# A decode kernel for grouped-query attention beside a Mish layer: no critical section at the start, and the first load of wq shared by two queues

## The chip, the cores and the metric

The kernel runs on one core of a Trainium2 chip. The core has five engines, each with its own instruction stream: TensorE (PE, matrix products; PEld are its weight loads), VectorE (DVE), ScalarE (ACT), GpSimd (POOL) and SyncE (SP). Sixteen DMA engines move data between HBM and the on-chip memory SBUF, which has 128 partitions; here SyncE and ScalarE issue DMAs, each on a queue of its own (q1 and q10 in the profile). PSUM holds the products of TensorE. The metric is the device time of one execution in microseconds (us), the median of the timed runs.

## The reference

For 8 sequences with one new token each: a layer norm of x (8 x 512), then the sum of x, an attention over a cache of 8192 positions, and a dense layer with the Mish activation. All is float32.

```python
def _A_ref(x, k_cache, v_cache, wq, wo):          # B=8, Sq=1, D=512
    Hq, Dh = 32, 128                               # 8 KV heads, 4 query heads each
    q = (x @ wq).reshape(B, Sq, Hq, Dh).transpose(0, 2, 1, 3)
    k = jnp.repeat(k_cache, rep, axis=1)           # k_cache, v_cache: (8, 8, 8192, 128)
    v = jnp.repeat(v_cache, rep, axis=1)
    scores = jnp.einsum("bhqd,bhkd->bhqk", q, k) * (Dh ** -0.5)
    p = softmax(scores, axis=-1)
    o = jnp.einsum("bhqk,bhkd->bhqd", p, v)
    return o.transpose(0, 2, 1, 3).reshape(B, Sq, Hq * Dh) @ wo

def _B_ref(x, w1, b1, w2):                         # F=1792
    h = jnp.einsum("bsd,df->bsf", x, w1) + b1
    return jnp.einsum("bsf,fd->bsd", h * jnp.tanh(softplus(h)), w2)

xn = layernorm(x)
return x + _A_ref(xn, k_cache, v_cache, wq, wo) + _B_ref(xn, w1, b1, w2)
```

The two caches are 268 MB each, and each of their elements is used once.

## The kernel before

**Tiling.** The work goes in 16 packs. A pack takes a pair of KV heads (`PAIRS` = 4) and two of the eight sequences (`PB` = 2, `NP` = 4). For each pack and each of its two sequences `b` one load brings K (128 partitions x 64 KB, 8.4 MB) and one brings V (as much). So the stream of the kernel is 64 such loads, and between them the weights: wq and wo in four pieces of 2 MB each, w1 and w2 with 3.7 MB each.

**Places in SBUF.** There are three big buffers. `kva` (place "a") holds 64 KB in each partition: w1 first, then the second K of pack 0, K(0,1), then the V's. `kvb` ("b") holds 80 KB, a quarter more than a load, so that the next K may be issued when three quarters of the one before have been read. `kvw` ("w") holds a piece of wq or wo.

**Order of the loads.** `plan` puts a load into a list, in the order in which the loads are to run; `pump` issues from the head of the list as long as the place of the head is free; `release`, called behind the last product that reads a place, frees it and calls `pump`. All loads in the list are issued by SyncE, which executes its DMAs in that order and waits ahead of each for a semaphore of the engine that read the place last. The order at the start is wq(0), w1, K(0,0), K(0,1), K(1,0), V(0,0), K(1,1), V(0,1), and so on. x (16 KB) and b1 (7 KB) are issued by ScalarE, on its own queue, at the head of the program.

**V(0,0).** One load is treated apart: `load_early`, called in the middle of the products of K(0,1), takes the head of the list, which is the second half of V(0,0), and issues it into the half of `kva` that these products have read by then. The first half of V(0,0) follows behind the last product of K(0,1).

**How the program is written out.** Every instruction is first recorded as an `Op` by `Program.add`, which works out from the regions read and written who has to wait for whom; `issue` (line 383 is the call in it that makes the instruction, so that nearly every row of the profile has that line) writes it out with its wait. `emit_first` writes out those instructions of the part ahead of the loop that stand before the first wait of their engine, among them the first DMAs and some memsets, inside a critical section of the framework (lines 1135 and 1138):

```python
    prog.prepare()
    with tc.tile_critical(no_gpsimd_drain=True):
        prog.emit_first()
    tc.close()
```

The framework puts a hand-over between engines at both ends of such a section, and a barrier at `tc.close()`. `emit` writes out the rest: what is ahead of the loop over packs 1 to 15, the loop for TensorE, VectorE and ScalarE, and the end.

**The start, step by step.** `setup` clears some tiles, computes the layer norm of x on VectorE (the first instruction that reads x is a reduction of `sc`, 8 x 512, into `st`), transposes it on TensorE and makes the selection matrices out of an identity. GpSimd copies the normalised x in another order, TensorE transposes that as well (`setup_w1`). `queries` multiplies with wq(0) into `H`; VectorE scales, transposes and copies it to `qc`, and `expand` makes `qT`, the weights for the scores. `mish` starts with the product of the selection `gsel` with b1 and goes on with w1; when its last product is done, `kva` is free for K(0,1). Then come `scores` of K(0,0), which are copied by ScalarE, `rows`, and `scores` of K(0,1). TensorE does all its products in that order.

Of the kernel before, what the change touches and what calls it, by code (L numbers as in the profile page):

```python
# [12 lines left out]
P = 128  # L13
# [9 lines left out]
G = 4  # L23
# [4 lines left out]
CC = D // P  # L28
# [11 lines left out]
HE = P // 2  # L40
V8 = PB * REP

KR = DH * 2 * NB // P
# [66 lines left out]
class Program:  # L110
# [260 lines left out]
            top[c] = max(n * self.unit[c], top.get(c, 0))  # L371
        return list(top.items())

    def issue(self, o, pack):
        engine = getattr(self.nc, o.engine)
        *first, last = self.values(o) or [None]
        for c, n in first:
            engine.wait_ge(self.sems[c], n)
        if o.method in ("settle", "relay"):
            got = engine.wait_ge(self.sems[last[0]], last[1])  # L380
        else:
            args, kw = (o.make(pack), {}) if o.make else (o.args, o.kw)
            got = getattr(engine, o.method)(*args, **kw)  # L383
            if last:
                got.wait_op(self.sems[last[0]], last[1], "sem-ge")
        if c := self.channel(o):
            got.then_inc(self.sems[c], o.unit)

    def emit_first(self):

        waiting = set()
        for o in self.ops:
            if o.waits:
                waiting.add(o.engine)
            if o.engine not in waiting and o.place[1] == "before":
                self.issue(o, o.pack)
                self.done.add(o)

    def emit(self):
        nc, issue, lower = self.nc, self.issue, self.lower  # L400
        for o in self.ops:
            if o not in self.done and (o.place[1] == "before" or o.engine not in LOOPED):
                issue(o, o.pack)
        for engine, parts in self.bodies():
            e = getattr(nc, engine)
            mine = [c for c in self.low if c[1] == engine]
            for c, n in (*self.low.items(), *self.early.items()):
                if c[1] == engine:
                    lower(engine, c, n)
            with e.Fori(FIRST, END) as pack:  # L410
                for ops, at in parts:
                    if name := ops[0].part:
                        with e.If_eq(e.to_reg(SOMETIMES[name](pack)), 0):
                            for o in ops:
                                issue(o, pack)
                            for c, k in self.drops.get((engine, "loop", at), {}).items():
                                lower(engine, c, max(k))
                        e.end_ifs()
                    else:
                        for o in ops:  # L420
                            issue(o, pack)
                for c in mine:
                    lower(engine, c, self.round[c])
            for o in self.ops:
                if o.place[1] == "after" and o.engine == engine:
                    issue(o, o.pack)
# [15 lines left out]
def kernel(  # L442
# [13 lines left out]
    prog = Program(nc)  # L456
    pe, dve, act, pool, sp = (getattr(prog, e) for e in ("tensor", "vector", "scalar", "gpsimd", "sync"))
# [12 lines left out]
    queue = []  # L470
    taken, landed, held = {}, {}, {}

    def rows_of(blocks):

        return blocks.rearrange("j p f -> (j p f)").rearrange("(p f) -> p f", p=P)

    def pump():

        while queue and taken.get(queue[0][1]) in (None, queue[0][0]):
            what, at, load = queue.pop(0)  # L480
            taken[at] = what
            landed[what] = load()

    def load_early():

        what, _, load = queue.pop(0)
        landed[what] = load()

    def release(what, relay=None):

        at = next(at for at, w in taken.items() if w == what)
        del taken[at]
        if relay:
            held[at] = [relay]
        pump()

    def plan(what, at, blocks, stream, part=(0, 1), lo=0):

        rows = rows_of(blocks)
        n = rows.shape[1]  # L500
        t = place[at][:, lo : lo + n]

        cols = slice(round(part[0] * n), round(part[1] * n))

        def load():
            sp.dma_start(t[:, cols], rows[:, cols], stream=stream, to="tensor", after=held.pop(at, ()))
            return t

        queue.append((what, at, load))

    sc = tile_of([P, 512], "sc")
    x_sb = sc[:B, :]
    act.dma_start(x_sb, x, stream="x", to="vector")

    acc = tile_of([P, D], "acc")
    b1_sb = acc[:G, :FG]
    act.dma_start(b1_sb, b1.rearrange("(g f) -> g f", g=G), stream="b1", to="tensor")

    def blocks_of(src, p, b):
        i, k = divmod(p, NP)  # L520
        lo = ((k * PB + b) * HKV + 2 * i) * NB
        return src[lo : lo + KN]
# [3 lines left out]
    def plan_k(p, b):  # L526
        blocks = blocks_of(kT, p, b)
        if (p, b) == (0, 1):
            plan(("k", p, b), "a", blocks, "k1")
        else:  # L530
            up[0] = KX * BW - up[0]
            plan(("k", p, b), "b", blocks, "k" if p else "k0", lo=up[0])

    def plan_v(p, b, at, stream="v", part=(0, 1)):
        plan(("v", p, b), at, blocks_of(v, p, b), stream, part)

    def plan_wq(i):
        plan(("wq", i), "w", wq[i * CC : (i + 1) * CC], "w")

    def plan_wo(i, stream="w", part=(0, 1)):  # L540
        plan(("wo", i), "w", wo[i * 4 : i * 4 + 4], stream, part)

    plan_wq(0)
    plan("w1", "a", w1, "w1")
    between = {}
    for i in range(1, PAIRS):
# [2 lines left out]
    for p in range(PACKS):  # L549
        for b in range(PB):  # L550
            plan_k(p, b)
            if (p, b) in between:
                what, i = between[p, b]
                (plan_wq if what == "wq" else plan_wo)(i)
            if p == 1 and b == 0:
                plan_v(0, 0, "a", "v1", (1 / 2, 1))
                plan_v(0, 0, "a", part=(0, 1 / 2))
            elif p > 0:
                plan_v(p - 1, b, "a")
    plan_v(PACKS - 1, 0, "b", "v0")  # L560
    plan_v(PACKS - 1, 1, "a", "va", (0, 3 / 4))
# [142 lines left out]
    def setup_w1(xs):  # L704
        for r in range(W1R):
            last = pe.transpose(
                M[:, 64 + r * B : 64 + (r + 1) * B], xs[:, r * P : (r + 1) * P], ident[:B, :B]
            )
        read = prog.relay("vector", "gpsimd", last)
        for t in range(2):  # L710
            dve.tensor_scalar(
                xw[:, :, t, :],
                M[:, 64 : 64 + W1R * B].rearrange("p (r b) -> p r b", r=W1R),
                half[:, t : t + 1],
                None,
                op0=ALU.mult,
            )

        pool.memset(pt, 0.0, after=[read], to="vector")
# [46 lines left out]
    def scores(b, k, order, first=False):  # L766

        t = qT[:, b].rearrange("p r u h -> p r (u h)")
        for r in order:
            if first and r == order[KR // 2]:  # L770
                load_early()
            for c in range(2):
                last = pe.matmul(
                    C[b][HE * c : HE * (c + 1), :],
                    t[:, r],
                    k[:, r * BW + c * 512 : r * BW + (c + 1) * 512],
                    start=(r == order[0]),
                    stop=(r == order[-1]),
                )
        read = prog.relay("scalar", "sync", last) if first else None  # L780
        act.copy(sc, C[b])
        return read
# [262 lines left out]

    prog.enter(0)
    pump()
    xs = setup()
    setup_w1(xs)
    read = queries(landed["wq", 0])  # L1050
# [5 lines left out]
    for p in range(PACKS):  # L1056
        prog.enter(p)
        for b in range(PB):
            k = landed.pop(("k", p, b))
            n = PB * p + b - (p > 0)  # L1060
            order = range(KR) if n % 2 == 0 else range(KR - 1, -1, -1)
            read = scores(b, k, order, first=(p, b) == (0, 1))
            release(("k", p, b), read)
            if p > 0 and b == 0:
# [21 lines left out]
            if (p, b) in between:  # L1086
                w = landed.pop(between[p, b])
# [16 lines left out]
    p = PACKS - 1  # L1104
# [27 lines left out]
    dve.tensor_copy(res, H[:, :P])  # L1132
    sp.dma_start(out, res, stream="out", to="sync")
    prog.prepare()
    with tc.tile_critical(no_gpsimd_drain=True):
        prog.emit_first()
    tc.close()
    tc.compile()
    prog.emit()
# [39 lines left out]
```

## Time and profile before

| | |
|---|---|
| median of 3 runs | 1304.92 us |
| lowest, highest run | 1304.13, 1305.15 us |
| profiled execution: time | 1304.17 us |
| profiled execution: span from first to last instruction | 1302.8 us |
| mean granted TensorE clock | 0.836 |
| TensorE / VectorE / ScalarE / GpSimd busy | 67% / 30% / 9% / 0% of the span |
| read from HBM | 561.01 MB, 431 GB/s over the span |
| chain that ended last | DMA 66%, PE 32%, DVE 1% |

The times of the profile are in us from the start of the span. "SPq" and "ACTq" are the sequencers of SyncE and ScalarE, which issue the DMAs; the duration in such a row is that of the issue, and the issue rows of the DMA view give the time from issue to landing. In a row of the timeline the start comes first, then the duration, the engine, the line and what is written from what; the bracket at the end tells how long the engine stood idle and who released it. "x16" is a count of instructions that were merged into one row. DMA packets are counted at their start, so a short stretch can show more than the engines can move.

### The profile page before, as it was taken

Reading aid. Unit: us, or ns where it says so; the run is one execution under the profiler, and the core shown is the slowest. Engines: PE = TensorE matmul, PEld = TensorE weight load, DVE = VectorE, ACT = ScalarE, POOL = GpSimd, SP = SyncE. Lnnn points to the kernel's source line nnn. Section 1 sums busy time; section 2 is a strip of 40 time slices with the busy share of each in tenths; the row PEclk is TensorE's granted clock in tenths of the full one; section 3 lists DMA queues with packets and bytes.
Section 4 is the critical chain, followed back from the end, with each engine's and each line's share of the span. In section 5 each row is a group of like instructions: output and inputs, shape, how many; then the busy total and the mean of one; then the engine's idle time right before and its main releaser. Section 6 shows DMA issues by size and latency. Waiting matters only on the chain.

```text
span 1302.8 us, 11368 instructions
## 1 busy us (share of the span) xinstructions
PE 874.2 (67%) x4814; PEld 279.6 (21%) x4814; DVE 389.9 (30%) x597; ACT 122.1 (9%) x294; POOL 4.8 (0%) x10
## 2 busy tenths in 40 slices
PE   4786657766667665686656686666876656766568
PEld 1221112212112221122211222111221221212113
DVE  6250504305051230521405133052320515115061
ACT  1020202001020100200102020020200102001020
POOL 1000000000000000000000000000000000000000
PEclk9887788887799877897887888778877779878889
DMA  9999999999999999999999999999999999999998
GB/s 402 447 423 436 429 439 431 431 437 431 439 429 441 425 443 425 434 433 437 431 433 437 420 450 427 443 425 443 423 441 429 437 431 433 435 431 439 429 432 363
DMA packets 11554, 561.22 MB, mean 431 GB/s; under 512 B 1292, under 2 KB 1424, under 8 KB 1560
## 3 DMA queue, kind: packets, MB, share of 16 engines
q1 hardware_dynamic: 11520, 561.06, 99.7%
q8 instruction: 7, 0.11, 0.0%
q10 hardware_dynamic: 24, 0.02, 0.0%
q14 instruction: 3, 0.02, 0.0%
HBM read 561.01 MB, written 0.07 MB: 431 GB/s over the span
## 4 chain that ended last, share of the span: by engine, by line
DMA 66%; PE 32%; DVE 1%; issue 0%; SPq 0%; ACT 0%; DVEq 0%
DMA kvb<-in_kT 65%; PE c L383 30%; DMA kvb<-in_w 2%; PE o L383 1%; DVE raw L383 0%; DVE pt L383 0%; SPq L383 0%; DVE os L383 0%; DVE nm L383 0%; PE s L383 0%; PE m L383 0%; PE h L383 0%; ACT sc L383 0%; DVE acc L383 0%; DVE nr L383 0%
## 5 line engine op out<-in xcount | busy, mean ns | idle before, releaser
L383 PE MATMUL c<-kvb,qT 128*64 128x512 f32 x1984 | 499.3, 667 | 330.9 <-DMA kvb<-in_kT 330.9
L383 PEld LDWEIGHTS c<-kvb,qT 128*64 128x64 f32 x1984 | 161.1, 154 | 669.1 <-issue 470.7
L383 PE MATMUL o<-kva,pt 128*32 128x512 f32 x1984 | 244.7, 650 | 24.7 <-DMA kva<-in_v 24.1
L383 DVE TENSOR_REDUCE nm<-s 128x1 f32<-128x1024 f32 x16 | 19.6, 1225 | 431.5 <-PE s L383 431.5
L383 DVE STREAM_TRANSPOSE raw<-wide 128x2048 f32<-128x2048 f32 x36 | 125.4, 3484 | 19.5 <-ACT wide L383 17.7
L383 ACT COPY sc<-c 128x512 f32<-128x512 f32 x32 | 18.7, 585 | 981.6 <-PE c L383 981.6
L383 PEld LDWEIGHTS o<-kva,pt 128*32 128x32 f32 x1984 | 65.8, 118 | 194.6 <-issue 151.9
L383 ACT ACTIVATE wide<-s,nms 128x512 f32<-128x512 f32 x128 | 88.0, 687 | 130.5 <-DVE nms L383 66.9
L383 DVE TENSOR_TENSOR oT<-m,rt 128x16 f32 (+1 forms) x17 | 3.0, 175 | 228.2 <-PE m L383 228.2
L383 DVE TENSOR_SCALAR os<-o,isel 128x128 f32<-128x128 f32 x32 | 11.2, 350 | 155.9 <-PE o L383 155.9
L383 DVE TENSOR_TENSOR pt<-raw 64x256 f32<-64x256 f32 x128 | 53.5, 418 | 1.9
L383 DVE TENSOR_TENSOR qT<-qc,bsel 128x1024 f32<-128x1024 f32 x34 | 40.2, 1222 | 17.5 <-PE s L383 17.4
L383 PE MATMUL s<-sc,csel 64*128 64x512 f32 x128 | 37.1, 657 | 8.5 <-ACT sc L383 7.1
L383 DVE TENSOR_TENSOR raw<-raw 128x1024 f32<-128x1024 f32 x32 | 39.2, 1225 | 2.9 <-DVE raw L383 0.2
L383 DVE SCALAR_TENSOR_TENSOR os<-o,isel,os 128x128 f32<-128x128 f32 x96 | 33.6, 351 | 3.4
L383 ACT ACTIVATION_READ_ACCUMULATOR wide<-s,nms 128x1 f32 x128 | 24.7, 193 | 0.0
L383 PE MATMUL m<-hsel,os 128*128 128x8 f32 x66 | 12.7, 265 | 10.6 <-DVE lsel L383 10.6
L383 PE MATMUL m<-ident,nm 128*1 128x128 f32 x16 | 4.4, 273 | 21.6 <-DVE nm L383 21.6
L383 DVE TENSOR_SCALAR wide<-h 128x512 f32<-128x512 f32 x16 | 11.1, 691 | 18.8 <-PE h L383 18.4
L383 PE MATMUL h<-kvw,xnT 128*64 128x512 f32 x64 | 16.5, 663 | 0.0
L383 PEld LDWEIGHTS m<-hsel,os 128*128 128x128 f32 x66 | 10.1, 193 | 25.3 <-issue 12.2
L383 PE MATMUL c<-kva,qT 128*64 128x512 f32 x64 | 14.0, 594 | 0.6 <-DMA kva<-in_kT 0.6
(92 smaller groups left out, 161.1 us busy)
## 6 DMA issues: line engine op xcount, KB each, us to landing
kvw<-in_wq SPq DMA_DIRECT2D x4, 2048.0 KB, 30.0
kva<-in_v SPq DMA_DIRECT2D x2, 4096.0 KB, 23.3
kvw<-in_wo SPq DMA_DIRECT2D x3, 2048.0 KB, 30.6
kva<-in_v SPq DMA_DIRECT2D x1, 6144.0 KB, 24.5
kva<-in_w SPq DMA_DIRECT2D x1, 3584.0 KB, 15.9
kva<-in_v SPq DMA_DIRECT2D x1, 2048.0 KB, 29.0
kvb<-in_w SPq DMA_DIRECT2D x1, 2048.0 KB, 13.9
kvw<-in_wo SPq DMA_DIRECT2D x2, 1024.0 KB, 18.1
```

The lines of the kernel that those rows point to most:

```text
L383: got = getattr(engine, o.method)(*args, **kw)
```

## The change

The critical section is gone: `emit_first` now writes out, without a section around it, only the DMAs that stand ahead of the first wait of their engine, and leaves the memsets to `emit`, behind `tc.close()`. The load of wq(0) is made of two DMAs, SyncE's for partitions 0 to 63 and ScalarE's for partitions 64 to 127, and x and b1 follow on ScalarE's queue. `load_early` is gone, and V(0,0) is one load like every other V, issued behind the last product of K(0,1).

```diff
--- before.py
+++ after.py
@@ -371,7 +371,7 @@
             top[c] = max(n * self.unit[c], top.get(c, 0))
         return list(top.items())
 
-    def issue(self, o, pack):
+    def issue(self, o, pack, own=None):
         engine = getattr(self.nc, o.engine)
         *first, last = self.values(o) or [None]
         for c, n in first:
@@ -383,17 +383,19 @@
             got = getattr(engine, o.method)(*args, **kw)
             if last:
                 got.wait_op(self.sems[last[0]], last[1], "sem-ge")
+        if own is not None:
+            own.add(got.ins.name)
         if c := self.channel(o):
             got.then_inc(self.sems[c], o.unit)
 
-    def emit_first(self):
+    def emit_first(self, tc):
 
         waiting = set()
         for o in self.ops:
             if o.waits:
                 waiting.add(o.engine)
-            if o.engine not in waiting and o.place[1] == "before":
-                self.issue(o, o.pack)
+            if o.engine not in waiting and o.method == "dma_start":
+                self.issue(o, o.pack, tc.no_tile_sem_insts)
                 self.done.add(o)
 
     def emit(self):
@@ -481,11 +483,6 @@
             taken[at] = what
             landed[what] = load()
 
-    def load_early():
-
-        what, _, load = queue.pop(0)
-        landed[what] = load()
-
     def release(what, relay=None):
 
         at = next(at for at, w in taken.items() if w == what)
@@ -494,7 +491,7 @@
             held[at] = [relay]
         pump()
 
-    def plan(what, at, blocks, stream, part=(0, 1), lo=0):
+    def plan(what, at, blocks, stream, part=(0, 1), lo=0, shared=False):
 
         rows = rows_of(blocks)
         n = rows.shape[1]
@@ -503,6 +500,10 @@
         cols = slice(round(part[0] * n), round(part[1] * n))
 
         def load():
+            if shared:
+                for queue, rest, name in ((sp, slice(0, HE), stream), (act, slice(HE, P), stream + "h")):
+                    queue.dma_start(t[rest], rows[rest], stream=name, to="tensor")
+                return t
             sp.dma_start(t[:, cols], rows[:, cols], stream=stream, to="tensor", after=held.pop(at, ()))
             return t
 
@@ -510,11 +511,9 @@
 
     sc = tile_of([P, 512], "sc")
     x_sb = sc[:B, :]
-    act.dma_start(x_sb, x, stream="x", to="vector")
 
     acc = tile_of([P, D], "acc")
     b1_sb = acc[:G, :FG]
-    act.dma_start(b1_sb, b1.rearrange("(g f) -> g f", g=G), stream="b1", to="tensor")
 
     def blocks_of(src, p, b):
         i, k = divmod(p, NP)
@@ -534,13 +533,13 @@
     def plan_v(p, b, at, stream="v", part=(0, 1)):
         plan(("v", p, b), at, blocks_of(v, p, b), stream, part)
 
-    def plan_wq(i):
-        plan(("wq", i), "w", wq[i * CC : (i + 1) * CC], "w")
+    def plan_wq(i, shared=False):
+        plan(("wq", i), "w", wq[i * CC : (i + 1) * CC], "w", shared=shared)
 
     def plan_wo(i, stream="w", part=(0, 1)):
         plan(("wo", i), "w", wo[i * 4 : i * 4 + 4], stream, part)
 
-    plan_wq(0)
+    plan_wq(0, shared=True)
     plan("w1", "a", w1, "w1")
     between = {}
     for i in range(1, PAIRS):
@@ -552,10 +551,7 @@
             if (p, b) in between:
                 what, i = between[p, b]
                 (plan_wq if what == "wq" else plan_wo)(i)
-            if p == 1 and b == 0:
-                plan_v(0, 0, "a", "v1", (1 / 2, 1))
-                plan_v(0, 0, "a", part=(0, 1 / 2))
-            elif p > 0:
+            if p > 0:
                 plan_v(p - 1, b, "a")
     plan_v(PACKS - 1, 0, "b", "v0")
     plan_v(PACKS - 1, 1, "a", "va", (0, 3 / 4))
@@ -767,8 +763,6 @@
 
         t = qT[:, b].rearrange("p r u h -> p r (u h)")
         for r in order:
-            if first and r == order[KR // 2]:
-                load_early()
             for c in range(2):
                 last = pe.matmul(
                     C[b][HE * c : HE * (c + 1), :],
@@ -1045,6 +1039,8 @@
 
     prog.enter(0)
     pump()
+    act.dma_start(x_sb, x, stream="x", to="vector")
+    act.dma_start(b1_sb, b1.rearrange("(g f) -> g f", g=G), stream="b1", to="tensor")
     xs = setup()
     setup_w1(xs)
     read = queries(landed["wq", 0])
@@ -1132,8 +1128,7 @@
     dve.tensor_copy(res, H[:, :P])
     sp.dma_start(out, res, stream="out", to="sync")
     prog.prepare()
-    with tc.tile_critical(no_gpsimd_drain=True):
-        prog.emit_first()
+    prog.emit_first(tc)
     tc.close()
     tc.compile()
     prog.emit()
```

In the program that results, SyncE begins with its half of wq, w1 and K(0,0) right behind the program's first barrier; ScalarE begins with its half of wq, x and b1. The products of `queries` wait for both halves.

## Prediction

> **What bounds the kernel now.** I read the page of the profile first, its DMA queues above all.
>
> ```profile
> span 1302.8 us, 11368 instructions
> ...
> q1 hardware_dynamic: 11520, 561.06, 99.7%
> ```
>
> One queue, SyncE's, keeps the sixteen DMA engines busy for 99.7% of the span and carries 561.06 MB. No compute engine comes near that. Whatever does not start these bytes sooner, or interrupt them, is worth nothing. The chain that ended last, in order of time, shows how the stream begins:
>
> ```profile
> 0.67 0.05 issue
> 0.72 0.01 SPq L1135
> 0.73 0.06 issue
> 0.80 0.03 SPq L1138
> 0.83 0.12 issue
> 0.95 0.38 SPq L383
> 1.34 0.05 issue
> 1.39 0.42 SPq L383
> 1.81 0.05 issue
> 1.86 36.01 DMA kvb<-in_kT
> ```
>
> SyncE leaves the program's first barrier at 0.67, passes the critical section's entry (L1135, L1138) and issues wq at 0.95, w1 at 1.39 and the first K at 1.86, which lands at 37.87. Everything that this change touches lies ahead of about 96 us; behind that the order of transfers is the old one. What a stretch of stream is worth, and what the start loses, the busy time by stage tells (us; x is a count; last columns PEclk, DMA share, GB/s):
>
> ```profile
> 1.50:2.00 0.50, 0.00 (x0) 0.00 (x0) 0.44 (x2) 0.00 (x0) 0.00 (x0) 1.00 0.42 98
> 1.90:5.90 4.00, 0.00 (x0) 0.00 (x0) 2.77 (x10) 1.28 (x1) 0.44 (x2) 1.00 1.02 335
> 45.00:50.00 5.00, 5.00 (x26) 1.63 (x24) 0.00 (x0) 0.00 (x0) 0.00 (x0) 1.00 1.00 433
> ```
>
> A full stretch moves 433 GB/s. The first bytes move about 1.0 us after the first issue (0.95 to some 2.0), and the first 4 us run at 335, so (433 - 335) / 433 x 4.0 = 0.9 us is lost while the stream gets up to speed.
>
> The profiled execution took 1304.17 us, 1.37 more than its span; the median of the three timed runs is 1304.92. I make the sum on 1304.17 and carry it to the median, 0.75 higher.
>
> **The change part by part.** *No critical section.* Between 0.67 and 0.95 the chain holds 0.28 us. The two named pieces and the issue gap between them, 0.72 to 0.83, belong to the section: 0.11 us. The 0.05 and 0.12 around them I take to be the way from any barrier to any DMA. So the stream starts 0.11 earlier, bounds 0 and 0.28. The section's other end holds back only VectorE, ScalarE and GpSimd (VectorE's first work on data, below, starts at 3.77). The closing barrier of the framework stays ahead of that work; now the first memsets stand behind it too, but they fit before x arrives, below.
>
> *wq from two queues.* The bytes are the same, and so are the sixteen engines. Two queues could overlap the slow first rows (at most the 0.9 us above), or each could pay for its own (0.9 more). I take 0, because SyncE's w1 and K are already issued behind wq before the first rows are through, so no engine lacks work either way; both ends stay for the range. The extra DMA costs nothing on SyncE, which issues nothing more until 25.35.
>
> *x and b1 behind half of wq.* This is the largest shift of work. Before, x is issued first:
>
> ```profile
> 0.91 0.62 ACTq L383 DMA_DIRECT2D sc<-in_x  x1
> ...
> 1.56 0.26 ACTq L383 DMA_DIRECT2D acc<-in_b  x1
> ...
> 3.77 0.67 DVE L383 TENSOR_REDUCE st<-sc 8x1 f32<-8x512 f32 x1 [1.01 <-PEq L1138]
> ...
> 12.70 5.54 PE L383 MATMUL h<-kvw,xnT 128*64 128x512 f32 x16
> ...
> 19.04 6.20 PE L383 MATMUL o<-kva,aT 128*8 128x448 f32 x64
> ...
> 24.34 2.36 DVE L383 TENSOR_TENSOR qT<-qc,bsel 128x1024 f32<-128x1024 f32 x2
> ...
> 25.35 0.33 SPq L383 DMA_DIRECT2D kva<-in_kT  x1
> ```
>
> That is the chain to watch in the timeline: layer norm of x on VectorE from 3.77, GpSimd's copies, the transposes, the queries at 12.70, the bias and w1 products to 25.24, and only then SyncE may issue the second K, since it goes where w1 was. All of it is one dependent chain, so it moves by as much as its first reduction does. How late x gets, the issues with their time to landing bound:
>
> ```profile
> kva<-in_w SPq DMA_DIRECT2D x1, 3584.0 KB, 15.9
> kvw<-in_wq SPq DMA_DIRECT2D x1, 2048.0 KB, 7.8
> ```
>
> wq lands at 0.95 + 7.8 = 8.75, w1 at 1.39 + 15.9 = 17.3. With 128 rows on 16 engines a row of w1 takes (17.3 - 8.75) / 8 = 1.07 us. If the two queues are served in turn, wq is complete near 8.75 as before, and x comes after one or two rows of w1: 9.8 to 10.9. The chain moves by 6.0 to 7.1 us, and the second K is issued at 31.4 to 32.5. Is that early enough? The small packets with which the sixteen engines close the first K, in the DMA view of 35.3 to 37.5 us, say when the engines run dry:
>
> ```profile
> DMA packets 32, 1.05 MB, mean 477 GB/s; under 512 B 16, under 2 KB 16, under 8 KB 16
> ```
>
> All 16 lie in that stretch. Less the 1.0 us from issue to first bytes, the second K must be issued by 34.3: 8.9 us after 25.35. So 2 to 3 us of cover are left, and the cost is 0. Past 8.9 us every further us empties engines, at full price. Nothing else on the way is near: the scores wait for the first K until 37.87, and the expanded queries, done at 24.34 + 2.36 = 26.7 before, are ready by 34.
>
> *V(0,0) in one load.* The second half used to be issued at half of the second K's products:
>
> ```profile
> 64.40 7.24 SPq L383 DMA_DIRECT2D kva<-in_v  x2
> ```
>
> That row merges both halves: the first at 64.40, the other ending at 71.64. Now both go out at the latter's 71.3. In front of them stands the third K, whose engines close in the DMA view of 74 to 76.2 us:
>
> ```profile
> DMA packets 45, 0.95 MB, mean 432 GB/s; under 512 B 16, under 2 KB 16, under 8 KB 16
> ```
>
> 71.3 + 1.0 = 72.3 is ahead of the first at 74: cost 0 with 1.7 us of cover. The order of bytes is unchanged, so the load lands when it did, and one issue on SyncE (0.33) is saved where it waits anyway. What the second K's products do to that is a rival.
>
> Sum: -0.11 + 0 + 0 + 0 = -0.11: 1304.06 for the profiled execution, 1304.8 for the median. Start alone gives bounds of -0.28 - 0.9 = -1.2 and +0.9.
>
> **The rivals.** *x comes too late and the stream runs dry (slower).* ScalarE's queue may not get its turn while SyncE's rows are queued. DMA views of 2.3 to 5.9 and of 5.9 to 7.1, queue rows, show b1, which was issued at 1.56:
>
> ```profile
> q1 hardware_dynamic: 67, 1.10, 77.6%
> ```
> ```profile
> q1 hardware_dynamic: 32, 0.52, 101.8%
> q10 hardware_dynamic: 8, 0.01, 1.7%
> ```
>
> ScalarE's queue (q10) got nothing for 3.6 us after b1's issue, while 67 rows of wq passed; that speaks for it. Against it: b1's 4 rows and their 4 small packets did get in at 5.9 to 7.1, with 32 packets of SyncE's in the same stretch and wq's rows not yet through (8.75); the row under way and 67 / 16, over four, per engine were ahead of it, not all that were queued. Were ScalarE's half served only when w1 is through, x would land at 17.3 plus 1.05 MB at 433 GB/s, 2.4 us: 19.7. Its reduction moves from 3.77 to 19.7, by 15.9; that is 7.0 past the 8.9, less 2.2 if only the last engine's end counts: 4.8 to 7.0 us slower, 1309.7 to 1311.9. It decides from x at 3.77 + 8.9 = 12.7 on, and costs over 2.6 us from 15.3 on. [...] The trace agrees that a queue waits several rows, but it counts five, which is why I give the rival 0.10 and not more.
>
> *The second K's products run slow and V(0,0) is late (slower).* TensorE's timeline and the busy time by stage:
>
> ```profile
> 57.27 13.95 PE L383 MATMUL c<-kva,qT 128*64 128x512 f32 x64 [0.59 <-DMA kva<-in_kT]
> ```
> ```profile
> 32.00:37.00 5.00, 0.00 (x0) 0.00 (x0) 4.83 (x6) 0.00 (x0) 0.00 (x0) 0.50 0.97 419
> ```
>
> The granted clock fell to 0.50 where TensorE idled. At 0.50 these 64 products would take 27.9 us instead of 13.95, V would be issued at 85.2, its bytes come at 86.2, and engines dry since 74 to 76 lose 10 to 12 us: about 1316. It decides from 1.7 us of delay. But TensorE will idle less ahead of 37.87 than before, not more, and the products start on a DMA whose place is kept: 0.03.
>
> *The two queues overlap the start:* up to 1.2 us faster, 1303.7. It speaks for it that the first 4 us run at 335; against, that the engines and not the issue set that pace. *Nothing comes of it:* the issue stays at 0.95, because the pieces named are the way into the program: 1304.9. Both lie within 0.2% of no change, and so does a start that costs 0.9.
>
> **How the numbers follow.** 0.2% is 2.6 us, about what a measurement of this kernel can tell from no change. The forecast has 0.60; overlap 0.12, nothing 0.06, a dearer start or a stream dry for under 2.6 us 0.05: together 0.83 within 0.2%. x too late 0.10 and V too late 0.03, with 0.01 for what I do not see: slower 0.14. Faster by 2.6 us would need nearly all of the 2.0 us before the first bytes and the 0.9 after: 0.03. The range goes from the lowest run less the bound, 1304.13 - 1.2 = 1302.9, to 1307.5, which takes in the highest run plus 0.9 (1306.05) and a stream dry for up to 2.6 us (1304.9 + 2.6). What is left out above and below is about 0.17.
>
> **What would show it.** Right: the first SyncE issue near 0.84, x's reduction at 10 to 11, the second K's issue at 31 to 33, the first K landing at 37.6 to 37.9 and the second at 57.1 to 57.3, the third at 76.4 to 76.6, V's one issue at 71, DMA at 9 in every slice. Wrong: the second K issued past 34.3, or the second or third K landing later than before by more than the first; V issued past 73; or a full stretch of stream that moves other than 433 GB/s.

## The result, and the profile after

The changed kernel takes 1311.14 us (median of 6 runs, 1310.21 to 1313.07) against 1304.53 (6 runs, 1303.98 to 1305.15): a ratio of 1.0053, 95% interval 1.0042 to 1.0063. It is slower by 0.5%, and lies above the range of the prediction. The profiled execution took 1310.21, 6.04 more than the one of before: 5.6 of it in the span (1308.4 against 1302.8), 0.4 outside. It is the fastest of the six; the others, up to 2.9 us slower, have no profile, and what makes them slower stays open.

The page of the changed kernel, slices and queues:

```profile
span 1308.4 us, 11354 instructions
...
GB/s 337 425 439 423 439 441 425 441 425 445 421 445 421 445 427 439 418 448 427 443 423 443 423 443 423 443 425 441 425 441 435 431 437 429 441 425 443 423 427 369
...
q1 hardware_dynamic: 11312, 560.01, 99.3%
q10 hardware_dynamic: 104, 1.07, 0.3%
```

The first slice of 32.7 us moves 337 GB/s; the others are as full as before. So the time went at the start. The busy time by stage there, after (last columns PEclk, DMA share, GB/s):

```profile
4.00:8.00 4.00, 0.00 (x0) 0.00 (x0) 1.19 (x5) 0.74 (x1) 0.16 (x2) 1.00 1.05 221
8.00:12.00 4.00, 0.00 (x0) 0.00 (x0) 0.00 (x0) 0.00 (x0) 0.00 (x0) 1.00 1.14 336
12.00:16.00 4.00, 0.00 (x0) 0.00 (x0) 0.00 (x0) 0.00 (x0) 0.00 (x0) 1.00 0.85 295
16.00:20.00 4.00, 0.00 (x0) 0.00 (x0) 1.61 (x4) 0.00 (x0) 0.00 (x0) 1.00 1.10 457
```

And the same first stage of before:

```profile
4.00:8.00 4.00, 0.00 (x0) 0.00 (x0) 3.39 (x12) 2.24 (x3) 0.33 (x2) 1.00 1.07 456
```

All sixteen engines are busy in both (share about 1), and yet they move half as much while wq's halves are under way. In the trace a 16 KB row of wq takes 0.611 us before once the stream runs (16 engines with such rows make 429 GB/s), and mostly about 1.28 us in the changed kernel's first half.

The issues of the changed kernel, with KB and us to landing, and its timeline:

```profile
kva<-in_w SPq DMA_DIRECT2D x1, 3584.0 KB, 20.4
kvw<-in_wq SPq DMA_DIRECT2D x1, 1024.0 KB, 8.5
kvw<-in_wq ACTq DMA_DIRECT2D x1, 1024.0 KB, 15.3
...
kvb<-in_kT SPq DMA_DIRECT2D x1, 40.3
...
kva<-in_kT SPq DMA_DIRECT2D x1, 22.0
```
```profile
0.73 0.56 SPq L383 DMA_DIRECT2D kvw<-in_wq  x1
0.74 0.57 ACTq L383 DMA_DIRECT2D kvw<-in_wq  x1
...
1.97 0.42 SPq L383 DMA_DIRECT2D kvb<-in_kT  x1
...
18.28 0.67 DVE L383 TENSOR_REDUCE st<-sc 8x1 f32<-8x512 f32 x1 [13.01 <-DMA sc<-in_x]
...
39.62 0.33 SPq L383 DMA_DIRECT2D kva<-in_kT  x1
```

The halves of wq land at 0.73 + 8.5 = 9.2 and 0.74 + 15.3 = 16.0, where the whole had landed at 8.75. The first K lands at 1.97 + 40.3 = 42.3 instead of 37.9, 4.4 late. And x, behind ScalarE's half, is reduced at 18.28 instead of 3.77, so the second K is issued at 39.62 instead of 25.35.

How much each of the two took is told by the small packets with which the sixteen engines close a load. The mean of their sixteen times in the trace, before and after: first K 35.95 and 40.34 (+4.4), second K 55.28 and 60.77 (+5.5), third K 74.71 and 80.22 (+5.5). So 4.4 us were lost up to the end of the first K, 1.1 between the first and the second, and nothing after that. The rows account for the 4.4: added up and shared among the sixteen engines, wq's rows took 8.9 us instead of 5.8, and w1's, some of which run between rows of ScalarE's half, 9.7 instead of 8.5. The 1.1 is a gap and a slow restart: the engines stood idle for 0.6 us on average, from 40.26 to 40.86, and their first rows of the second K then took 2.99 us instead of 2.42.

### The profile page after: what moved, and what is told of

It is laid out like the page before. It is cut to its first block, busy times and chain, and to the rows that moved or that the text cites. A ratio compares the mean times of both kernels' runs of the same rounds, so it can differ in the third digit from the quotient of the medians.

```text
span 1308.4 us, 11354 instructions
## 1 busy us (share of the span) xinstructions
PE 870.1 (66%) x4814; PEld 279.7 (21%) x4814; DVE 390.0 (30%) x597; ACT 122.1 (9%) x294; POOL 4.8 (0%) x10
## 3 DMA queue, kind: packets, MB, share of 16 engines
q10 hardware_dynamic: 104, 1.07, 0.3%
## 4 chain that ended last, share of the span: by engine, by line
DMA 61%; PE 31%; DVE 1%; issue 0%; ACT 0%; SPq 0%; DVEq 0%
DMA kvb<-in_kT 59%; PE c L383 30%; DMA kvb<-in_w 2%; PE o L383 1%; DVE raw L383 1%; DVE pt L383 0%; ACT wide L383 0%; SPq L383 0%; DVE os L383 0%; DVE nm L383 0%; PE s L383 0%; PE m L383 0%; PE h L383 0%; ACT sc L383 0%; DVE acc L383 0%
## 5 line engine op out<-in xcount | busy, mean ns | idle before, releaser
L383 PE MATMUL o<-kva,pt 128*32 128x512 f32 x1984 | 238.6, 637 | 24.0 <-DMA kva<-in_v 23.5
L383 DVE STREAM_TRANSPOSE raw<-wide 128x2048 f32<-128x2048 f32 x36 | 125.6, 3489 | 19.5 <-ACT wide L383 17.7
## 6 DMA issues: line engine op xcount, KB each, us to landing
kva<-in_w SPq DMA_DIRECT2D x1, 3584.0 KB, 20.4
```

## The experiments

Theory P: a load of 64 neighbouring partitions moves at half the rate. Theory Q: two queues with big loads hold each other up. Theory L: x comes late, and all else follows. Theory V: V(0,0) in one load, or the missing section, costs the time.

**Whole wq (e1)**, and x first:

```diff
-    plan_wq(0, shared=True)
+    plan_wq(0)
...
-    pump()
     act.dma_start(x_sb, x, ...)
     act.dma_start(b1_sb, ...)
+    pump()
```

> The changed kernel with wq(0) in one load of 128 partitions on SyncE's queue again and x and b1 at the head of ScalarE's; still no critical section, and V(0,0) in one load. Theory P (a load of 64 neighbouring partitions moves at half rate): the first K lands at 37.7 to 37.9 as before, DMA 4 to 8 us at 430 GB/s or more, time 1304.4 +- 0.5. Theory Q (two big queues hold each other up) and theory L (x comes late, so the second K does): the same, 1304.4. Theory V (V(0,0) in one load or the missing section costs the time): 1309 to 1311.

Measured: 1304.38 (11 runs) against 1304.16, ratio 1.0003 (0.9994 to 1.0012); the first K lands at 37.54, and 4 to 8 us move 483 GB/s. The whole loss is in the shared wq and in what stands behind it on ScalarE's queue. Theory V is out.

**Shared by columns (e2)**: two queues as in the change, but each with all 128 partitions.

```diff
-                for queue, rest, name in ((sp, slice(0, HE), stream), (act, slice(HE, P), stream + "h")):
-                    queue.dma_start(t[rest], rows[rest], stream=name, to="tensor")
+                for queue, rest, name in ((sp, slice(0, n // 2), stream), (act, slice(n // 2, n), stream + "h")):
+                    queue.dma_start(t[:, rest], rows[:, rest], stream=name, to="tensor")
```

> The changed kernel, with wq(0) shared by the two queues by columns: SyncE's the first half of each of 128 rows, ScalarE's the second half; x and b1 still behind ScalarE's half. Theory P: 4 to 8 us at 420 GB/s or more, first K landing at 37.7 to 38.2; x still behind rows of SyncE's w1, so its reduction at 10 to 15 instead of 3.8 and the second K issued at 32 to 37; time 1304.4 to 1306. Theory Q: as slow as the changed kernel up to the first K (42), 1309 to 1311. Theory L: between, by the time of the second K's issue, with the first K on time.

Measured: 1304.92 against 1304.16, ratio 1.0005 (0.9996 to 1.0014). Stage and issues:

```profile
4.00:8.00 4.00, 0.00 (x0) 0.00 (x0) 0.71 (x4) 0.21 (x1) 0.00 (x0) 1.00 1.14 482
```
```profile
10.90 0.67 DVE L383 TENSOR_REDUCE st<-sc 8x1 f32<-8x512 f32 x1 [6.16 <-DMA sc<-in_x]
```
```profile
33.26 0.33 SPq L383 DMA_DIRECT2D kva<-in_kT  x1
```

Two queues with the same bytes run at full rate (482 GB/s, 456 before), so Q is out. x comes at 10.90 and the second K is issued at 33.26, inside the 34.3 of the prediction: an x that is late by this much costs next to nothing (the closing packets of the first and second K lie 19.5 us apart, where 19.3 separate them before).

**Both halves on one queue (e3)**, x first:

```diff
-                for queue, rest, name in ((sp, slice(0, HE), stream), (act, slice(HE, P), stream + "h")):
+                for queue, rest, name in ((sp, slice(0, HE), stream), (sp, slice(HE, P), stream + "h")):
```

> The changed kernel with both halves of wq(0), partitions 0 to 63 and 64 to 127, on SyncE's queue one behind the other; x and b1 at the head of ScalarE's queue, so x is early. Theory P: 4 to 8 us near 211 GB/s, first K landing at 41.5 to 42.8, second K issued before 31, nothing dry, time 1308.3 to 1309.5. Theory Q: 1304.4, first K at 37.8. Theory L: 1304.4.

Measured: 1308.96 against 1304.16, ratio 1.0038 (1.0024 to 1.0051). First K's issue and landing, then the stages:

```profile
2.60 39.67 DMA kvb<-in_kT
```
```profile
4.00:8.00 4.00, 0.00 (x0) 0.00 (x0) 3.62 (x11) 1.23 (x1) 0.58 (x3) 1.00 0.97 203
```
```profile
8.00:12.00 4.00, 0.61 (x4) 0.55 (x4) 2.70 (x13) 1.49 (x2) 0.71 (x1) 1.00 1.06 230
```

With one queue and an early x (second K issued at 27.98) the half rate is there, the first K lands at 42.27, 4.4 late as in the changed kernel, and nothing runs dry. That is P by itself, 4.8 us in the time of the kernel, and it refutes Q and L as the main cause.

**x first, two queues (e4)**: the change with only the `pump()` moved behind x and b1, as in e1's diff.

> The changed kernel with x and b1 at the head of ScalarE's queue, ahead of its half of wq(0). Theory P: first K landing at 41.5 to 42.8 as in the changed kernel, x's reduction near 5.5 (behind the memsets), second K issued before 32 (wq's second half lands near 16.1), nothing dry at 40 to 44 us; 1308.3 to 1309.8, so 1.3 to 2.8 faster than the changed kernel, which is the price of the late x. Theory Q: the same landing, the same price. Theory L: 1304.4.

Measured: 1311.92 against 1304.16, ratio 1.0055 (1.0041 to 1.0069). This was missed: it was to be faster than the changed kernel by the price of the late x, and it is as slow. The issues:

```profile
kva<-in_w SPq DMA_DIRECT2D x1, 3584.0 KB, 22.9
kvw<-in_wq SPq DMA_DIRECT2D x1, 1024.0 KB, 7.8
kvw<-in_wq ACTq DMA_DIRECT2D x1, 1024.0 KB, 20.5
...
kvb<-in_kT SPq DMA_DIRECT2D x1, 42.6
```
```profile
8.00:12.00 4.00, 0.61 (x4) 0.55 (x4) 2.81 (x15) 1.41 (x2) 1.31 (x2) 1.00 1.01 252
12.00:16.00 4.00, 1.02 (x8) 0.92 (x8) 2.27 (x9) 0.00 (x0) 2.66 (x2) 1.00 1.07 281
16.00:20.00 4.00, 0.00 (x0) 0.00 (x0) 0.00 (x0) 0.00 (x0) 0.00 (x0) 1.00 1.04 289
```

ScalarE's half, issued behind x and b1, now alternates with SyncE's w1 up to 21 us, and the stream stays below 300 GB/s from 8 to 20 us. w1's rows, which write all partitions, take 1.49 us on average there instead of 1.06. So the rows of the half also hold up the full rows that run between them: wq's rows together took 3.4 us per engine more than before and w1's 3.4, where the changed kernel has 3.1 and 1.2. The first K lands 6.7 late (44.6), nothing runs dry, and what x gave back was paid again. The second K was issued at 35.04, but behind a K that ended at 42 to 44.

**Even and odd partitions (e5)**: 64 rows per queue as in the change, only others.

```diff
...
-                for queue, rest, name in ((sp, slice(0, HE), stream), (act, slice(HE, P), stream + "h")):
+                for queue, rest, name in ((sp, slice(0, P, 2), stream), (act, slice(1, P, 2), stream + "h")):
```

The lines left out change how `Program.add` counts the regions of such a load, so that neither half waits for the other.

> The changed kernel with the halves of wq(0) dealt out in turn: SyncE's queue loads the even partitions, ScalarE's the odd ones, 64 rows each, as many per queue as in the changed kernel; x and b1 still behind ScalarE's half. Theory P1 (the price is that 64 neighbouring partitions are written at a time): 4 to 8 us at 420 GB/s or more, first K landing near 37.4 as with the columns, second K issued at 32 to 35, 1304.3 to 1305.5. Theory P2 (the price is in a load of 64 rows, four per DMA engine, whichever they are): 4 to 8 us near 211 GB/s, first K at 42, 1309.5 to 1312.

The profiled execution took 1304.51, with

```profile
4.00:8.00 4.00, 0.00 (x0) 0.00 (x0) 1.19 (x5) 0.74 (x1) 0.16 (x2) 1.00 1.10 468
```

so the price hangs on which 64 rows a load takes and not on their number: each row of 16 KB takes 0.61 us again, even or odd. But the timed runs lay between 1304.51 and 1308.44, median 1306.44 against 1304.19, ratio 1.0020 (1.0011 to 1.0029): more than expected. The profiled execution is the fastest of them, and in it x was not late:

```profile
8.17 0.67 DVE L384 TENSOR_REDUCE st<-sc 8x1 f32<-8x512 f32 x1 [2.91 <-DMA sc<-in_x]
...
30.24 0.33 SPq L384 DMA_DIRECT2D kva<-in_kT  x1
```

Here ScalarE's half went first (its rows start at 2.07 to 5.25, SyncE's at 5.05 to 7.77), while in the changed kernel SyncE's did (2.10 to 5.86, ScalarE's 6.71 to 13.19).

**The same with x first (e9)**, the `pump()` moved as before:

> Even and odd partitions from two queues as in the run before, with x and b1 at the head of ScalarE's queue. It asks why the timed runs with even and odd partitions lay between 1304.5 and 1308.4 while the profiled one showed a stream as full as before. If x comes late in some executions (its place behind ScalarE's half varies) and the second K with it: x early takes it away, 1304.2 to 1304.8 with a spread near 1 us. If it is the load in two interleaved halves that varies: a spread of some 4 us again, median near 1306.

Measured: 1304.59 against 1304.08, ratio 1.0006 (0.9997 to 1.0015); ten of eleven runs between 1303.94 and 1305.42, one at 1306.87. An early x takes away most of it. So x's place behind ScalarE's half may differ between executions, but that is not shown: the slower executions have no profile, and e4, whose x is early too, varies by 2.8 us.

Beside e4 this run says more. The two kernels differ in nothing but which partitions a half takes (and in the bookkeeping for it), and in both ScalarE's half alternates with w1. The stage in which e4 moves 252 GB/s:

```profile
8.00:12.00 4.00, 0.61 (x4) 0.55 (x4) 2.84 (x15) 1.38 (x2) 1.35 (x2) 1.00 1.09 470
```

w1's rows take 1.06 us here, where they took 1.49, and the time is 1304.59 where it was 1311.92.

**The first K in halves (e7)**: the kernel before, a load four times as large.

```diff
+            if what == ("k", 0, 0):
+                for rest, name in ((slice(0, HE), stream), (slice(HE, P), stream + "h")):
+                    sp.dma_start(t[rest], rows[rest], stream=name, to="tensor")
+                return t
```

> The kernel before, with the first K (8.39 MB) in two loads on SyncE's queue, partitions 0 to 63 and then 64 to 127. This makes the disputed load four times as large. Theory P: at 211 GB/s instead of 433 the K takes 39.8 us instead of 19.4, lands at 57 to 59 and everything behind it comes 19 to 21 us later: 1323 to 1325. Theory Q (two queues): 1304.2, since there is one queue. Theory L (late x): 1304.2, since x is early.

Measured: 1326.50 against 1304.19, ratio 1.0170 (1.0155 to 1.0186), 22.3 us for four times the bytes of wq(0).

```profile
20.00:36.00 16.00, 6.94 (x72) 1.67 (x64) 14.84 (x19) 0.58 (x1) 0.00 (x0) 0.80 1.00 206
```

At 206 GB/s instead of 433, 8.39 MB take 40.7 instead of 19.4 us, 21.3 more. The scores start at 60.03 instead of 37.91, 22.1 later; the expectation was 1 to 3 us low. It took 211 GB/s for the half rate, and it left out the K behind: of its first rows, those that ran while other engines still had rows of the half took 2.8 to 4.1 us instead of 2.42, and it closed 20.4 us after the first K where 19.3 lie between them before.

**x late, wq whole (e8)**: x and b1 on SyncE's queue behind w1.

```diff
             sp.dma_start(t[:, cols], rows[:, cols], stream=stream, to="tensor", after=held.pop(at, ()))
+            if what == "w1":
+                sp.dma_start(x_sb, x, stream="x", to="vector")
+                sp.dma_start(b1_sb, ...)
...
-    plan_wq(0, shared=True)
+    plan_wq(0)
```

> The changed kernel with wq(0) whole on SyncE's queue, and x and b1 on SyncE's queue between w1 and the first K: x is as late as in the changed kernel and no load is halved. x's reduction at 17 to 18.3, first K landing at 37.4 to 37.9, second K issued at 38.6 to 39.9. The engines run dry from 35.3 to 37.4 on until about 1.0 us after that issue, so theory L's price by itself: 2.3 to 5.5 us, 1306.5 to 1309.7. If a late x cost nothing: 1304.4.

Measured: 1310.14 against 1304.19, ratio 1.0045 (1.0031 to 1.0059). Timeline and stages:

```profile
17.33 0.67 DVE L383 TENSOR_REDUCE st<-sc 8x1 f32<-8x512 f32 x1 [12.01 <-DMA sc<-in_x]
```
```profile
37.00:38.00 1.00, 1.00 (x16) 0.33 (x12) 0.96 (x2) 0.00 (x0) 0.00 (x0) 1.00 0.00 0
38.00:39.00 1.00, 1.00 (x12) 0.11 (x4) 0.97 (x2) 0.00 (x0) 0.00 (x0) 1.00 0.00 0
39.00:40.00 1.00, 0.52 (x6) 0.23 (x4) 1.00 (x2) 0.00 (x0) 0.00 (x0) 1.00 0.00 0
40.00:41.00 1.00, 1.00 (x8) 0.46 (x6) 1.00 (x2) 0.00 (x0) 0.00 (x0) 1.00 2.49 852
```

This is the prediction's first rival by itself: the second K is issued at 39.21, its first bytes come at 40.18, and the stream stands still in between. The engines' closing packets of the second K come at 60.37 on average instead of 55.10 (e1), 5.3 later. In the changed kernel the same lateness cost only 1.1, because the first K, 4.4 late itself, covered the rest.

**No critical section, nothing else (e6).**

```diff
...
-    with tc.tile_critical(no_gpsimd_drain=True):
-        prog.emit_first()
+    prog.emit_first(tc)
```

The lines left out are those of the change in `issue` and `emit_first`.

> The kernel before without the critical section, and nothing else: whole wq(0) on SyncE, x and b1 at the head of ScalarE's queue, V(0,0) in two loads. First SyncE issue at 0.74 instead of 0.95. If the earlier start is worth what it shows: 0.2 faster than before, 1304.0 +- 0.3. If it is given back outside the span, as with the whole wq: 1304.2 +- 0.3, with a span near 1302.3 and some 1.8 us outside it instead of 1.4.

Measured: 1304.39 (11 runs) against 1304.19, ratio 1.0002 (0.9993 to 1.0011). SyncE's first issue is at 0.74, and the profiled span is 1302.2 instead of 1302.8. But the time outside the span is 1.72 us (median of the 11) where the kernel before has 1.37 (median of 21), and 1.66 to 1.74 in every other kernel without the section; e7, which has it, shows 1.35. What the earlier start gives, the part outside the span takes back.

## Why the prediction was wrong

*wq from two queues* is the step that failed: the term was taken at 0 with bounds of 0.9 either way, and it measured 4.4 in the changed kernel's first K (by itself, in e3, 4.4 there and 4.8 in the time). The sentence at fault is "The bytes are the same, and so are the sixteen engines." The engines were the same and were busy; what had changed was which partitions a load filled at a time. The two bounds were for the first rows of a start, not for the rate of a load of 64 partitions, and no row of before showed one, since every load but x and b1 had 128. The runs show that the rate hangs on which 64 rows a load takes: 203 to 221 GB/s for 64 neighbours (4 to 8 us in e3 and in the changed kernel), 468 in the same stretch of e5, with the even partitions and the odd ones. Why neighbours are slow was not shown: partition p takes the p-th row of the piece in HBM, so a load of 64 partitions also reads other rows, and no run changes the partitions alone. Nor does a run load other sets of 64 than neighbours, even and odd ones. The prediction weighed how the queues share the engines and not which partitions a load fills.

*x behind half of wq*: the chain was right, its inputs were not. x's reduction came at 18.28 instead of 9.8 to 10.9, because ScalarE's half landed at 16.0 and not at 8.75; the second K was issued at 39.62 instead of 31.4 to 32.5. The cover of 8.9 us grew by the 4.4 that the first K was late, to 13.3; the second K's issue moved by 14.3; 1.0 should be lost, and 1.1 was. So the rival "x comes too late", given 0.10, did happen, as the smaller part of the loss. That 8.9 is its threshold is borne out by e2 (moved by 7.9, 0.2 lost) and by e8 (moved by 13.9, 5.3 lost for 5.0 past the threshold).

*The queues' turns*: served in turn, as the prediction read from b1, x would come at 9.8 to 10.9, and e2 has it at 10.9. In the changed kernel SyncE's four rows per engine went ahead of all of ScalarE's, and these then alternated with w1's nearly row by row; that, and rows of 1.07 us on average instead of 0.61, made ScalarE's half as late as 16.0.

*No critical section*: SyncE's issue moved by 0.21 instead of 0.11, and the time did not move (e6). The time outside the span, which grew, was not in the sum.

*V(0,0) in one load*: right. e1 and e6 differ in it, and take 1304.38 and 1304.39. *The second K's products run slow*, the other rival, came true in a small part and cost nothing: the products took 15.43 us instead of 13.95, but V was issued at 77.22, still ahead of the third K's first closing packet at 79.76.

Nothing was found that beats the kernel before: the best two variants (e1, e6) cannot be told from it.

## What to carry to other kernels

A DMA engine that is busy is not a DMA engine at full rate (from 4 to 8 us a busy share of 1.05 with 221 GB/s in the changed kernel, 1.07 with 456 before): before splitting a load, ask which partitions each part takes, and split by columns (482 GB/s in e2), or leave it whole. In a kernel that a stream of loads bounds, follow the chain that allows the next load and count its cover; a delay was free here up to the point at which the queue runs empty (7.9 us cost 0.2 in e2), and beyond it cost its full length and a slow restart (5.0 us past that point cost 5.3 in e8). A start that moves inside the span has to be looked for in the time outside it as well (in e6 the span shrank by 0.6 us, and the time outside it grew by 0.35).

## What the runs showed of the hardware

A load of partitions 0 to 63 or 64 to 127 moves 203 to 221 GB/s on sixteen busy engines, against 433 with all 128 (the changed kernel, e3, e7); even or odd partitions, and halves of columns, keep the full rate (468 and 482 in a stage that shows 456 before). Whether it is the writing of these partitions or the reading of their rows that halves the rate, the runs do not separate. Rows of such a half slow full-width rows between which they run: w1's took 1.49 us instead of 1.06 on average (e4), and 1.06 between rows of odd partitions (e9). A stream that ran dry needs about 1 us from the next issue to its first bytes (39.21 to 40.18 in e8), as at the start of the kernel before (0.95 to 1.99), and its first rows take longer (2.95 us instead of 2.42 in e8).
